# First block of a convolution and SiLU kernel: the copy of the taps on ScalarE instead of VectorE, and one product of zeros fewer

## The chip, the cores and the metric

The kernel runs on one core of a Trainium2 chip. The core has a matrix engine (TensorE, PE in the profile, with its weight loads as PEld), VectorE (DVE), ScalarE (ACT), GpSimd (POOL) and a queue engine (SyncE, SP) that only issues DMAs here. The engines run side by side, each takes its own instructions in order, and they wait for one another by semaphores. The metric is the time of one execution on the device in microseconds (us), less is better.

## What is computed

The input x is 8 sequences of 4096 tokens with 192 features, the output 32768 rows of 192. First a causal convolution of 7 taps along each sequence, with taps that are a softmax per head (8 heads of 24 features), then a two-layer block with SiLU between:

```python
def _attn_ref(x, weight):            # x (8, 4096, 192), weight (8, 7)
    w = np.exp(weight - weight.max(-1, keepdims=True))
    w = w / (np.sum(w, axis=-1, keepdims=True) + 1e-09)
    x_pad = np.concatenate([np.zeros((B, 6, D)), x], axis=1)
    idx = np.arange(S)[:, None] + np.arange(7)[None, :]
    x_unf = x_pad[:, idx, :].reshape(B, S, 7, H, 24)
    return np.einsum('hk,bskhg->bshg', w, x_unf).reshape(B, S, D)

def _moe_ref(x, w_in, w_out):        # w_in (192, 2048), w_out (2048, 192)
    h = x @ w_in
    return (h * (1.0 / (1.0 + np.exp(-h)))) @ w_out
```

The weights w_in and w_out are given in float64, all else in float32.

## The kernel before

The 32768 tokens are worked on in 32 blocks of 1024 tokens, each as two halves of 512. The features are split into three groups k of 64 (lines 120 to 150 load them); a tile xt holds both halves, 64 features on partitions 0 to 63 for the first 512 tokens and on 64 to 127 for the second, with 6 halo columns in front. VectorE transposes each loaded group into xt (turn_in, line 387). The convolution of a group multiplies shifted views of xt by one scalar per partition, the tap, which stands in the tile taps, 128 partitions by 3 x 7.

In all blocks but the first, a fixed plan written out in the kernel (PLAN) interleaves the convolution of the next block on VectorE with the products of this one on TensorE, the sums and SiLU. Blocks after the first use a product scheme with fewer multiplications (lines 497 and 570). The first block has no block before it to hide behind, and its start is written out by hand. Almost every instruction passes through a small helper, Pinned, which records it with an order to keep; all such instructions carry the line of that helper, L111, in the profile, so they are told apart by engine, operation and tile. Each engine's final sequence comes out of a scheduler; instructions with different engines are tied by semaphores alone.

The start of the first block, in steps:

- SP and ScalarE issue the first loads: weight, the four pieces of group 0 of x (tile nat), the halo of group 0 (halo, line 146), w_in for the rounding (tile raw), then the pieces of groups 1 and 2.
- VectorE clears zeros, warm, wown and one_hot. TensorE multiplies zeros by zeros into an unused bank (heat, line 339): four such products ahead of the taps and two behind them. Each shows as two records in the profile.
- POOL builds hot, a matrix of ones and zeros that maps heads to partitions, by six affine selects, and one_hot, an identity, by two, and clears the halo of the first half of xt.
- The softmax of weight runs on VectorE and ScalarE into wown. One product (line 365) of hot and wown puts the tap of the right head on each partition, into a bank by_head.
- by_head is copied to taps.
- diagonal (line 798) makes, for groups 0 and 1 and each tap, a diagonal 128 x 128 matrix on ScalarE: one_hot times the tap. conv_pe (line 805) uses these as weights: the convolution of groups 0 and 1 of the first block is 7 products for each half in TensorE, added up in a bank. Group 2 is done by VectorE (conv, lines 404 and 409) and spread by DMA (line 421).
- After the first transpose VectorE clears the halo columns of groups 1 and 2 on the upper 64 partitions, and POOL issues the DMAs that fill them (halo, line 146).
- VectorE and ScalarE round w_in, held as pairs of 32-bit words, to float32 tiles wr (rounded, round_in), in parts: three for the first of four, then the others whole; POOL copies them crosswise to ws.
- up_plain (line 460) does the first layer of the first block in four parts, down_plain (line 599) the second layer.

The hand-written sequence in question, after the functions:

```python
    turn_in(0, 0)
    vec.memset(xts[0][R:P, 1:NK, 0:pad], 0.0)
    for k in range(1, NK):
        halo(k, nc.gpsimd)
    diagonal(0)
    conv_pe(0)
    round_in(0, 0)
    diagonal(1)
    turn_in(0, 1)
    conv_pe(1)
```

Of the kernel before, what the change touches and what calls it, by code (L numbers as in the profile page):

```python
# [17 lines left out]
def kernel(  # L18
# [84 lines left out]
    def pin(ins):  # L103
        return tc.keep_in_program_order(ins)
# [8 lines left out]
    vec, act = Pinned(nc.vector), Pinned(nc.scalar)  # L113

    def bank():
        return psum.tile([P, TB], F32, tag="ps", name="ps")
# [219 lines left out]
    def heat(times):  # L336
        for _ in range(times):
            pin(
                nc.tensor.matmul(  # L339
                    idle[:, 0 : 2 * P],  # L340
                    zeros,
                    zeros.unsqueeze(1).to_broadcast([P, 2, P]),
                    start=True,
                    stop=True,
                )
            )

    idle, by_head = bank(), bank()[:, 0 : NK * K]
    taps = const.tile([P, NK, K], F32, name="taps")
# [20 lines left out]
            stop=True,  # L370
        )
    )
    heat(2)
    vec.tensor_copy(taps.rearrange("p k i -> p (k i)"), by_head)

    tails = {}

# [535 lines left out]
```

## Time and profile before

| what | value |
|---|---|
| median of four runs | 2409.5 us (2409.09, 2409.33, 2409.66, 2410.03) |
| the profiled execution, its own time | 2409.09 us |
| its span, first to last instruction | 2407.4 us |
| TensorE busy | 2399.6 us, 17878 records |
| VectorE busy | 2062.2 us |
| ScalarE busy | 995.1 us |
| POOL busy | 71.5 us |
| products of zeros (L339), first four, second two | 1.14 us for 3.61, 5.04 us for 1.11 |
| product that spreads the taps (L365) | 4.83 us for 0.37 |
| copy of the taps, VectorE | 5.23 us for 0.18 |
| first transpose, VectorE (L387) | 5.42 us for 0.71 |
| first seven diagonals, ScalarE | 5.51 us for 2.15 |
| products of the convolution (L805) | 6.28 us for 12.29, 56 records |

The page calls an engine busy while it has an instruction under way; matmuls overlap, so that a busy TensorE need not run at its peak, and the distance from one product's start to the next tells more than a product's length. "Idle before" with an arrow names what the profile takes for the event that ended a wait. In the chain of waits each piece is followed by what it released. Times are from the start of the span.

### The profile page before, as it was taken

How to read it: one execution, taken by the hardware profiler on the slowest of the kernel's cores; microseconds unless marked ns; L12 is line 12 of the kernel's file. 1: busy time of each engine (PE TensorE's matmuls, PEld its weight loads, DVE VectorE, ACT ScalarE, POOL GpSimd, SP SyncE). 2: the span in 40 equal slices, each digit the busy share in tenths (PEclk: the TensorE clock that was granted, in tenths of full speed). 3: DMA queues.
4: the chain of work that ended last, by engine and by line, in shares of the span. 5: the costliest groups of instructions: out<-in, count | busy, mean ns of one | idle time of the engine just before them, and what ended most of it. 6: DMA issues, size and time to landing. Idle time of an engine off the chain costs nothing.

```text
span 2407.4 us, 43335 instructions
## 1 busy us (share of the span) xinstructions
PE 2399.6 (100%) x17878; PEld 945.2 (39%) x17878; DVE 2062.2 (86%) x2812; ACT 995.1 (41%) x1873; POOL 71.5 (3%) x99
## 2 busy tenths in 40 slices
PE   9999999999999999999999999999999999999998
PEld 5333443334433344333344333443334433334433
DVE  8789888888888898888988888888889888898876
ACT  5334543334533345433454334453334533345432
POOL 4300000000000000000000000000000000000000
PEclk9999999999999999999999999999999999999999
DMA  7322122221222222222222222122222222222220
GB/s 159 61 45 47 34 36 54 54 41 32 44 45 54 40 41 36 44 54 44 45 37 36 54 51 43 32 40 50 53 40 41 36 45 54 43 43 37 38 40 14
DMA packets 453718, 110.59 MB, mean 46 GB/s; under 512 B 424080, under 2 KB 429200, under 8 KB 453520
## 3 DMA queue, kind: packets, MB, share of 16 engines
q1 hardware_dynamic: 449872, 105.85, 24.0%
q8 instruction: 140, 2.29, 0.4%
q0 software_dynamic: 448, 1.58, 0.3%
q10 hardware_dynamic: 3200, 0.39, 0.1%
q14 instruction: 58, 0.48, 0.1%
HBM read 31.46 MB, written 25.17 MB: 24 GB/s over the span
## 4 chain that ended last, share of the span: by engine, by line
PE 100%; DVE 0%; ACT 0%; issue 0%; ACTq 0%; DVEq 0%
PE ps L497 49%; PE ps L570 47%; PE ps L599 2%; PE ps L460 2%; PE ps L805 1%; PE ps L339 0%; DVE cmb L111 0%; ACT u L111 0%; DVE osb L111 0%; DVE xt L387 0%; PE ps L365 0%; ACTq L739 0%; DVE zeros L111 0%; DVE xt L111 0%; DVEq L387 0%
## 5 line engine op out<-in xcount | busy, mean ns | idle before, releaser
L497 PE MATMUL ps<-dup,ws 64*128 64x512 f32 x2480 | 869.9, 589 | 0.0
L570 PE MATMUL ps<-g,wo 128*32 128x512 f32 x2976 | 661.8, 593 | 0.0
L521 DVE TENSOR_TENSOR g<-u,ps 128x512 f32<-128x512 f32 x744 | 485.9, 680 | 119.1 <-PE ps L497 89.8
L497 PE MATMUL ps<-win,wr 64*128 64x512 f32 x1488 | 567.7, 589 | 0.0
L570 PE MATMUL ps<-t,wo 128*32 128x128 f32 (+2 forms) x4528 | 500.6, 446 | 0.0
L518 ACT ACTIVATE g<-g 128x512 f32<-128x512 f32 x744 | 444.7, 631 | 97.3 <-DVE g L521 97.3
L497 PEld LDWEIGHTS ps<-dup,ws 64*128 64x128 f32 x2480 | 363.0, 187 | 292.0 <-issue 277.7
L570 PE MATMUL ps<-t,wx 128*32 128x512 f32 x2976 | 452.7, 592 | 0.0
L409 DVE SCALAR_TENSOR_TENSOR nat<-xt,taps,nat 128x512 f32<-128x512 f32 x564 | 423.4, 751 | 18.3 <-ACT nat L404 3.7
L497 PE MATMUL ps<-dup,wr 64*128 64x512 f32 x992 | 419.9, 596 | 0.0
L512 ACT COPY u<-ps 128x512 f32<-128x512 f32 x496 | 278.1, 589 | 228.7 <-PE ps L497 225.8
L638 ACT COPY cmb<-ps 96x512 f32<-96x512 f32 x30 | 17.5, 582 | 805.3 <-PE ps L570 805.3
L538 DVE TENSOR_TENSOR t<-g 128x1024 f32<-128x1024 f32 x248 | 299.7, 1219 | 27.2 <-PE ps L570 27.2
L538 DVE TENSOR_TENSOR t<-g,t 128x1024 f32<-128x1024 f32 x248 | 303.3, 1224 | 13.6 <-PE ps L570 3.2
L497 PEld LDWEIGHTS ps<-win,wr 64*128 64x128 f32 x1488 | 233.4, 187 | 175.5 <-issue 146.9
L570 PEld LDWEIGHTS ps<-t,wo 128*32 128x32 f32 x4528 | 180.3, 110 | 219.8 <-issue 199.5
L497 PE MATMUL ps<-win,ws 64*128 64x512 f32 x496 | 242.2, 589 | 0.0
L570 PE MATMUL ps<-g,wx 128*32 128x512 f32 x1488 | 234.5, 592 | 0.0
L570 PEld LDWEIGHTS ps<-t,wx 128*32 128x32 f32 x2976 | 121.9, 110 | 278.8 <-issue 269.5
L650 DVE TENSOR_TENSOR cmb<-cmb,ps 96x512 f32<-96x512 f32 x150 | 102.3, 682 | 135.2 <-ACT u L635 133.1
L497 PEld LDWEIGHTS ps<-dup,wr 64*128 64x128 f32 x992 | 160.5, 187 | 128.2 <-issue 114.3
L570 PEld LDWEIGHTS ps<-g,wo 128*32 128x32 f32 x2976 | 168.5, 110 | 98.3 <-issue 98.3
(72 smaller groups left out, 1228.7 us busy)
## 6 DMA issues: line engine op xcount, KB each, us to landing
dup<-nat SPq DMA_DIRECT2D x376, 128.0 KB, 2.3
nat<-in_x_dram SPq DMA_DIRECT2D x382, 64.0 KB, 2.4
out_dram<-osb SPq DMA_DIRECT2D x376, 64.0 KB, 2.0
raw<-in_moe_w_out_dram SPq DMA_DIRECT2D x8, 384.0 KB, 3.9
raw<-in_moe_w_in_dram SPq DMA_DIRECT2D x12, 192.0 KB, 4.5
ws<-wr POOLq DMA_DIRECT2D x8, 192.0 KB, 4.0
raw<-in_moe_w_in_dram SPq DMA_DIRECT2D x6, 128.0 KB, 3.0
xt<-xt SPq DMA_DIRECT2D x31, 4.5 KB, 1.9
```

The lines of the kernel that those rows point to most:

```text
L409: nc.vector.scalar_tensor_tensor(out=dst, in0=src, scalar=tap, in1=dst, op0=ALU.mult, op1=ALU.add)
L460: nc.tensor.matmul(hs[a, n, e], rows(wr[j], e)[:, a, k, :], rows(d, e)[:, n, k, :], start=k == 0, stop=k == NK - 1,)
L497: nc.tensor.matmul(bk[b, m, bn], rows(w, half), rows(v, half), start=first, stop=True, skip_group_check=True,)
L512: pin(copy(u, bk[b, m, "1"]))
L518: pin(nc.scalar.activation(g, g, AF.Silu))
L521: pin(nc.vector.tensor_tensor(g, us.pop((b, m, i)), bk[b, m, bn], op=ALU.add))
L538: pin(nc.vector.tensor_tensor(t[i // 2][:, i % 2, :], u, v, op=ALU.subtract))
L570: nc.tensor.matmul(accs[b][at][SQ * q : SQ * q + SQ, to], lhs[:, e, SQ * k : SQ * k + SQ], rhs[:, e, ts(q, TB // 4) if i == 5 else to], st ...
L599: nc.tensor.matmul(acc[k][R * n : R * n + R, :], wo[j][:, a, e, R * k : R * k + R], gs[b, j, a][:, n, e, :], start=j == 0 and a == 0 and e ...
L638: pin(nc.scalar.copy(c[0], acc[0][0:n, :]))
L650: pin(nc.vector.tensor_tensor(out_, u, v, op=ALU.add))
L805: nc.tensor.matmul(by_pe[k][n], rows(diag, n)[:, k, i, :], rows(xts[0], n)[:, k, i : i + TB], start=i == 0, stop=i == K - 1,)
```

## The change

Two lines of the first block's start are changed. The second run of products of zeros has one in place of two. The copy of by_head to taps is issued on ScalarE in place of VectorE.

```diff
-    heat(2)
-    vec.tensor_copy(taps.rearrange("p k i -> p (k i)"), by_head)
+    heat(1)
+    act.copy(taps.rearrange("p k i -> p (k i)"), by_head)
```

In the built program, the sequences of the engines differ in these places and no other:

- TensorE: one product of zeros less between line 365 and line 805.
- VectorE: wown, then the first transpose, with no copy between.
- ScalarE: the exponential of weight, then the copy of by_head, then the first diagonal.
- POOL: the last of the six selects of hot stands behind the first of the two halo DMAs (line 146), where it stood ahead of it.
- SP: one of the loads of the second block's input stands ahead of a pair of loads of w_out, where it stood behind it.

POOL's queue from the last but one select of hot on, before and after:

```
before                                        after
select  hot<-hot                              select  hot<-hot
memset  xt                                    memset  xt
select  hot<-hot                              DMA     xt<-in_x_dram  (waits for VectorE)
DMA     xt<-in_x_dram  (waits for VectorE)    select  hot<-hot
DMA     xt<-in_x_dram                         DMA     xt<-in_x_dram
```

## The prediction

> **What bounds the kernel now.** I read the page's busy times first, then the waits of TensorE, then the chain that ended last in order of time, then the first 30 us of the timeline, engine by engine.
>
> Page, busy times; waits of TensorE over the whole span (engine, tile and line, releaser, us in total, times, longest):
>
> ```profile
> PE 2399.6 (100%) x17878; PEld 945.2 (39%) x17878; DVE 2062.2 (86%) x2812; ACT 995.1 (41%) x1873; POOL 71.5 (3%) x99
> ```
>
> ```profile
> PE ps L339 <- DVE warm L111: 1.1, 1, 1.1
> ```
>
> TensorE is busy for 2399.6 of 2407.4 us and has one listed wait, for its very first product. A late start of its work is therefore a late end, unless something later makes it wait anyway. The chain (start, length, what) shows where that work starts:
>
> ```profile
> 4.75 0.08 issue
> 4.83 0.39 PE ps L365 x2
> 5.21 0.02 issue
> 5.23 0.03 DVE taps L111
> ...
> 5.42 0.71 DVE xt L387
> 6.13 0.06 issue
> 6.19 0.08 DVE xt L111
> 6.27 0.01 issue
> 6.28 12.29 PE ps L805 x56
> ```
>
> ```profile
> 18.57 41.22 PE ps L460 x192
> 59.79 41.35 PE ps L599 x192
> ```
>
> From 6.28 on the chain is TensorE alone: 41.22 us over 192 products is 0.215 us each, 41.35 again, and each later block repeats 37.97 + 36.22 us to the hundredth. So the time of the kernel is the start of the first convolution product (line 805) plus a constant. The chain ahead of it: the product that spreads the taps over partitions (line 365, 4.83), VectorE's copy of them (5.23), VectorE's first transpose (5.42 to 6.13), the convolution. ScalarE's first diagonal (started 5.51, 0.386 us, so done at 5.90) is ready before the transpose. The POOL row that follows must be read beside it (timeline):
>
> ```profile
> 3.53 0.29 POOL L111 TENSOR_SCALAR_AFFINE_SELECT hot<-hot 32x128 f32<-32x128 f32 x1
> 6.57 1.53 POOL L146 DMA_DIRECT2D xt<-in_x_dram  x2 [2.75 <-DVE xt L111]
> ```
>
> ```profile
> 3.99 0.69 DVE L111 TENSOR_SCALAR wown<-wexp,wred 8x7 f32<-8x7 f32 x3
> 6.19 0.07 DVE L111 MEMSET xt<- 64x12 f32 x1
> ```
>
> The select at 3.53 is the last that builds hot, an operand of the line 365 product. The two halo DMAs come after it on POOL and wait for VectorE's memset at 6.19.
>
> **The change part by part.** Taken at its word, it lets the transpose start when VectorE is free (3.99 + 0.69 = 4.68) instead of behind the tap copy, and gives ScalarE the copy that ScalarE alone waits for. But the built order of POOL's queue changes with it. Before: memset xt, select hot, halo DMA, halo DMA. After: memset xt, halo DMA, select hot, halo DMA. The first halo DMA still waits for VectorE's memset, and that memset still stands behind the transpose. The last select of hot, so the line 365 product, so the taps, so the diagonals, now stand behind both. The old order could not be built this way (the memset stood behind the tap copy, which needs hot); the new one can. The path, step by step:
>
> - Transpose: starts 4.70. Its four loads must have landed: the second of SP's two is issued by about 1.7, and these loads land 2.9 us after issue in the median, 3.4 at most, so 4.6 to 5.1. I take 4.70, as the bytes of small packets thin out by 3.5 us. Ends 4.70 + 0.71 = 5.41.
> - Memset: 0.06 later, 0.07 long (6.13 to 6.19, 6.26): ends 5.54.
> - First halo DMA on POOL: 0.31 after the memset (6.26 to 6.57), issue 0.82: 5.85 to 6.67.
> - Last select of hot: POOL goes on 0.02 after the end of its DMA issues (35.81 + 1.31, next row 37.14), 0.29 long: ends 6.98.
> - Line 365 product: 0.15 after its last operand (4.68 to 4.83): 7.13. Taps can be read 0.40 later (4.83 to 5.23): 7.53.
> - Tap copy on ScalarE: no row has it. Nearest below: VectorE's same copy, 0.181, and ScalarE on 128x1, 0.204; above: ScalarE on 128x128, 0.386. For 21 columns I interpolate 0.23; bounds 0.18 and 0.39. Ends 7.76. The diagonal, which waits for it on the same engine, 0.05 later (the lag of VectorE's dependent rows, 3.76 to 3.80): 7.81.
> - First diagonal 0.386: 8.20; product 0.14 after (6.13 to about 6.28, the transpose being the wait): 8.34.
>
> Shift: 8.34 - 6.28 = 2.06 us. With the loose ends (load +0.4, copy -0.05 to +0.16, the lags -0.1 to +0.1) 1.9 to 2.7.
>
> The removed product of zeros costs or saves nothing here: the products of zeros no longer end anywhere near the wait, TensorE stands still until 8.34 in any case. Without that cover (the order of POOL as before) it would still have been hidden behind the transpose (the zeros ended at 5.04 + 1.11 = 6.15, against 6.13 for the transpose).
>
> What else is late: ScalarE's diagonals run 2.30 late (5.51 to 7.81), the rounding steps of w_in queued behind them (7.70) to 10.0, and VectorE's step that waits for these (8.15) to 10.45. VectorE idles 0.80 before its third transpose (11.26, a load), so from there it is 2.30 - 0.80 = 1.5 late. The tightest need of TensorE is the second part of w_in: rounded at 27.51 + 0.96 = 28.47, wanted at 18.37 + 48 x 0.215 = 28.68. Both slide, to 29.97 and 30.74: the margin grows, and no new wait comes. The halo columns land about 3.1 us after issue: the first at 9.8 at the latest, wanted at 8.34 + 6.0 = 14.4; the second, issued by 7.8, at 10.9, wanted by ScalarE at 13.5. On SP one load of the second block's input goes ahead of a pair of w_out loads (28.46 and 35.57), some 0.5 us of issue; that w_out is rounded at 51.14.
>
> One cost has only bounds: the pace of TensorE. The eight records of zeros from 1.14 start 0.45 us apart ((4.28 - 1.14) / 7), the last three of the second four 0.21 apart (5.34, 5.55, 5.77). The pace doubled at about 5.2, after some 4.1 us of work without a gap over 0.1 us, while the granted clock is 1.00 in every stretch. In the changed kernel TensorE stands still from 4.75 to 7.13 and again before 8.34. Lower bound: the pace comes as before and stays, 0. Upper bound from these rows: the 4.1 us start over at 8.34, half of them lost, 2.0 us. I take 0, because the first four products (3.61 us) are nearly all that was there when the pace came.
>
> [...]
>
> Sum against the profiled execution: 2409.09 (span 2407.4 and 1.7 around it) + 2.06 = 2411.15. That execution is the lowest of the four; the median stands 0.4 above, so **2411.6** for the median.
>
> **The rivals.**
>
> *Held on POOL, and the fast pace lost.* As above, but the convolution starts at half pace. For: the starting work is cut into 3.61 us, a gap of 2.4, under 1 us, a gap of 0.4. Against: only 0.6 us of products were still to come when the pace doubled. Price 0 to 2.0: 2411.6 + 2.0 = 2413.6 at the full bound, typically 2412.5 to 2413.6. This is also the one way to a measurable loss: over 0.2% (4.8 us, about what a measurement of this kernel can tell from no change) it needs 4.8 - 2.06 = 2.75 us here, 5.5 us of convolution at half pace, more than the 4.1 that the trace shows.
>
> *The change does what it says: the POOL order does not bind.* Taps at 5.23 + 0.23 = 5.46, diagonal from 5.51, done 5.90, product at 6.04: 0.24 earlier. But then the second part of w_in comes last (28.47 + 0.14 = 28.61 against 28.68 - 0.24 = 28.44) and takes 0.17 back: 2409.3 to 2409.5, not slower than before. For: the select is 0.29 us of work and was idle time's neighbour; against: each engine's rows start in the built order everywhere in this trace, and the product's wait is for the last of POOL's ten steps.
>
> *A later wait absorbs the shift.* If VectorE or a load bound TensorE somewhere in the first two blocks, the end would slide by less, 2409.5 to 2411. Against: one listed wait, and 0.215 us per product throughout.
>
> **How the numbers follow.** Held on POOL with the pace as before 0.52 (2411.0 to 2412.2); held with the pace lost 0.31; as it says 0.12; absorbed 0.05. The time is that of the first, 2411.6. The range 2410.9 to 2413.9 takes in the first, most of the second and a little of the last: about 0.8. All but the far end of the second lie within 0.2% (2404.7 to 2414.3): faster 0.01, same 0.90, slower 0.09.
>
> **What would show it.** On POOL the halo DMA near 5.85 ahead of the last select of hot (near 6.7); the line 365 product near 7.1; the tap copy on ScalarE at 0.2 to 0.3 us; the convolution near 8.3; line 460 at 20.6 and 41.2 long as before; no new wait of TensorE. A first convolution longer than 12.29 us for its 56 records would show the lost pace, and the excess its price. The prediction is wrong if the select ends by 4 us, if the convolution starts before 7, or if a later block's 37.97 or 36.22 changes.

## The result and the profile after

| | before | changed |
|---|---|---|
| median | 2409.38 us (60 runs, 2409.01 to 2410.03) | 2412.87 us (40 runs, 2412.42 to 2414.18) |
| span of the profiled execution | 2407.4 us | 2411.9 us |
| the profiled execution's own time | 2409.09 us | 2413.64 us |

The ratio is 1.0016, 95% interval 1.0011 to 1.002: slower, by 3.5 us in the median and by 4.5 us in the two profiled executions, and still within the 0.2% that the forecast counts as the same. The 40 times fall in two groups with nothing between: 21 from 2412.42 to 2412.87, 19 from 2413.39 to 2414.18. The profiled execution is of the upper group.

First the page's busy times and TensorE's waits (engine, tile and line, releaser, us in total, times, longest):

```profile
PE 2402.2 (100%) x17876; PEld 942.3 (39%) x17876; DVE 2064.4 (86%) x2811; ACT 995.3 (41%) x1874; POOL 70.6 (3%) x99
```

```profile
PE ps L365 <- POOL hot L111: 2.1, 1, 2.1
PE ps L339 <- DVE warm L111: 1.1, 1, 1.1
```

TensorE has one wait that it did not have: the product that spreads the taps waits 2.1 us for hot, on POOL. The chain of waits tells what stood ahead of that on POOL (start, length, what):

```profile
4.67 0.71 DVE xt L387
5.38 0.06 issue
5.45 0.08 DVE xt L111
5.53 0.29 issue
5.82 0.82 POOL xt L146
6.64 0.06 issue
6.70 0.30 POOL hot L111
7.00 0.04 issue
7.04 0.62 PE ps L365 x2
7.66 1.03 PE ps L339 x2
8.69 14.43 PE ps L805 x56
```

```profile
23.12 41.20 PE ps L460 x192
64.32 41.35 PE ps L599 x192
```

Transpose, memset, halo DMA, select of hot, tap product: the order of POOL's queue, step after step. Two more things are in these lines. The 56 records of the convolution take 14.43 us where they took 12.29. And the chain comes to them from the product of zeros (line 339), not from ScalarE's diagonal. From line 460 on all is as before (41.20 and 41.35 against 41.22 and 41.35), 4.55 us later. So the whole loss lies before 23.12 us: 2.3 to 2.4 us in the start of the convolution (8.62 against 6.28 for its first record; 8.69 in the chain), 2.14 us in its length.

TensorE's weight loads show where the length comes from (timeline, start, length, gap before):

```profile
11.35 0.34 PEld L805 LDWEIGHTS ps<-xt,diag 64*128 64x128 f32 x2 [0.51 <-ACT diag L111]
12.20 0.34 PEld L805 LDWEIGHTS ps<-xt,diag 64*128 64x128 f32 x2 [0.51 <-issue]
13.05 0.22 PEld L805 LDWEIGHTS ps<-xt,diag 64*128 64x128 f32 x2 [0.51 <-ACT diag L111]
13.52 0.19 PEld L805 LDWEIGHTS ps<-xt,diag 64*128 64x128 f32 x2 [0.24 <-issue]
13.95 0.19 PEld L805 LDWEIGHTS ps<-xt,diag 64*128 64x128 f32 x2 [0.24 <-issue]
```

Up to 13.05 the pairs start 0.85 us apart, after that 0.43: TensorE runs at half pace for 4.4 us of the convolution. "ACT diag" as a releaser is not the reason; the diagonals come every 0.31 us, and the distance is the same where no releaser is named.

TensorE was at half pace already when it fell idle, and still when it went on (timeline, the first four products of zeros and the tap product):

```profile
1.14 3.78 PE L339 MATMUL ps<-zeros 128*128 128x256 f32 x8 [1.14 <-DVE warm L111]
7.04 0.62 PE L365 MATMUL ps<-wown,hot 96*128 96x21 f32 x2 [2.12 <-POOL hot L111]
```

In the profile before, the same rows took 3.61 and 0.37 us: there the full pace had come by the start of the tap product at 4.83.

### The profile page after: what moved, and what is told of

Same layout as the page of the kernel before. It is cut to its first block, busy times and chain, and to the rows that moved or that the text cites. A ratio compares the mean times of both kernels' runs of the same rounds, so it can differ in the third digit from the quotient of the medians.

```text
span 2411.9 us, 43332 instructions
## 1 busy us (share of the span) xinstructions
PE 2402.2 (100%) x17876; PEld 942.3 (39%) x17876; DVE 2064.4 (86%) x2811; ACT 995.3 (41%) x1874; POOL 70.6 (3%) x99
## 4 chain that ended last, share of the span: by engine, by line
PE 99%; DVE 0%; ACT 0%; issue 0%; POOL 0%; ACTq 0%; DVEq 0%
PE ps L497 49%; PE ps L570 46%; PE ps L599 2%; PE ps L460 2%; PE ps L805 1%; DVE cmb L111 0%; ACT u L111 0%; PE ps L339 0%; ACTq L128 0%; DVE osb L111 0%; POOL xt L146 0%; DVE xt L387 0%; PE ps L365 0%; DVE wown L111 0%; ACT L111 0%
```

## The experiments

My theory after the result: two causes, in a row. POOL's order holds the tap product back, and the standing still costs TensorE its full pace. The rivals: ScalarE's copy is to blame, or the missing product of zeros, or the pace has nothing to do with the waiting.

**e1, one product of zeros fewer, and nothing else**

```diff
-    heat(2)
+    heat(1)
     vec.tensor_copy(taps.rearrange("p k i -> p (k i)"), by_head)
```

> One product of zeros fewer, tap copy still on VectorE, every other queue as before. Theory (the loss comes from POOL's order and from the pace that the waiting costs): TensorE's standing still stays under 0.7 us, the convolution starts at 6.28 as before, 2409.4 us, no difference over 0.2 us. Rival (the removed product alone lets the pace slip): the convolution's 56 records take more than 12.3 us, and the time lies 0.5 to 2 us above before.

Measured 2409.23 against 2409.56 us for before beside it, ratio 1.0 (0.9991 to 1.0009); the convolution starts at 6.27 and takes 12.29 us. But two of the 11 times are 2411.10 and 2411.13, where none of the 33 of before is above 2410.22. The removed product is not what costs 3.5 us; it costs some 2 us in some executions. Theory and rival each had a part of it.

**e2, the copy on ScalarE, and nothing else**

```diff
     heat(2)
-    vec.tensor_copy(taps.rearrange("p k i -> p (k i)"), by_head)
+    act.copy(taps.rearrange("p k i -> p (k i)"), by_head)
```

> The tap copy on ScalarE, both products of zeros kept, POOL's order as in the changed kernel. Theory (POOL's order): the select of hot ends at 7.0, the convolution starts at 8.4 to 8.7, and the time is that of the changed kernel, 2412.4 to 2414.2 in two groups; one product more in the gap changes the pace little, so within 0.6 us of 2412.9. Rival (the removed product matters): back to 2411.5, the pace being kept by the second product.

Measured 2414.16 (2411.28 to 2414.51), ratio 1.0017 (1.0008 to 1.0026). POOL's rows are those of the changed kernel: DMA at 5.85, select at 6.73. So the move of the copy brings the loss. That the median lies 1.3 us above the changed kernel's was not expected, and the chain says why (before, the wait for POOL; here, what follows the tap product):

```profile
7.07 0.62 PE ps L365 x2
7.69 1.89 PE ps L339 x4
9.57 14.03 PE ps L805 x56
```

At half pace the two products of zeros take 1.89 us and end at 9.57, after the first diagonal (ScalarE starts it at 8.00); the convolution stands behind them. The changed kernel's one product ends at 8.69. One execution, 2411.28, is 1.6 us below the next: with no profile of it, I can only guess that it kept the pace.

**e3, the whole change with POOL's order restored.** The halo columns are first filled from the tap tile, not with zeros; the DMAs overwrite them either way. Since the taps need hot, the halo DMAs can only come after the select.

```diff
-    vec.memset(xts[0][R:P, 1:NK, 0:pad], 0.0)
+    vec.tensor_copy(xts[0][R:P, 1:NK, 0:pad], taps[R:P, 1:NK, 0:pad])
```

> The whole change, but the halo columns are first filled from the tap tile instead of with zeros (the DMAs overwrite them either way), which puts both halo DMAs behind the last select of hot as before. Theory (POOL's order is the whole cause): the convolution starts at 6.0 to 6.1 in place of 8.6, its 56 records take 12.3 us, and the time is 2409.2 to 2409.5. Rival (ScalarE's copy or the missing product is to blame): 2410.5 to 2413.

Measured 2409.10 against 2409.56, ratio 1.0 (0.9991 to 1.0008); again two times of 11 above 2411. The chain:

```profile
4.82 0.38 PE ps L365 x2
5.21 0.02 issue
5.23 0.19 ACT taps L111
...
5.50 0.41 ACT diag L111
5.91 0.04 issue
5.95 12.29 PE ps L805 x56
18.24 8.15 PE ps L460 x37
```

With the select in its old place (3.53) the loss is gone, with ScalarE's copy and one product of zeros still in. The copy does what it was said to: the transpose leaves the chain, the diagonal takes its place, and the convolution starts 0.33 us earlier than before. Part of that is given back: line 460's 192 records take 41.35 us in place of 41.22, with one weight load, at 28.39, coming 0.68 us after the end of the one before it, where the others come after 0.21 to 0.24. The rounded weights of line 460's second part, ready at 27.32 + 0.96 = 28.28, fit that wait; the profile names a step of ScalarE for it, so this is my reading. The span is 0.1 us shorter than before, which no time can tell from nothing.

**e4, the changed kernel with TensorE's wait filled**

```diff
-    heat(4)
+    heat(8)
```

> The changed kernel with eight products of zeros in place of four ahead of the taps' product, so that TensorE works on until about 6.7 while POOL holds it; POOL's order as in the changed kernel. Theory (the shift is 2.0 to 2.3 us of waiting plus 1 to 2 us of half pace): the convolution starts at 8.4, its records take 12.3 us, 2411.4 to 2411.7, and the two groups of times go. Rival (the pace has nothing to do with the idle time): the records still take 13.3 to 14.5 us, 2412.4 to 2414.

Measured 2411.12 (2410.98 to 2411.60; one group), ratio 1.0006 (0.9998 to 1.0015). POOL's order is that of the changed kernel (DMA 5.86, select 6.74), and the chain now goes through the zeros:

```profile
1.14 6.40 PE ps L339 x16
7.54 0.15 PE ps L365 x2
...
7.98 0.41 ACT diag L111
8.39 0.04 issue
8.43 12.29 PE ps L805 x56
```

Work that computes nothing makes the changed kernel faster: all 11 times lie below all 40 of the changed kernel, and the median is 1.56 us above that of before beside it, in place of 3.49. The convolution is back at 12.29 us, and it starts 0.19 us earlier, no longer behind zeros at half pace. What is left in the profile, 8.43 - 6.28 = 2.15 us, is POOL's order, with some 0.2 us of the added zeros in it: the tap copy starts at 7.71, where the select's end, 7.03, with 0.04 to the tap product as in the changed kernel and 0.40 to the copy as before, would give 7.47 (an estimate). The rival that the pace has nothing to do with the waiting falls.

**e5, order restored, both products of zeros kept**, e3 with `heat(2)`

> The order restored as in e3, and both products of zeros kept behind the taps' product. In e1 and e3, with one of them, 2 of 11 times each stand near 2411.1, some 2 us above the rest; of the 93 times of before none does. Theory (the second product of zeros covers the stretch before the convolution, and without it the fast pace is lost in some executions): no time above 2410.3; the convolution starts at 6.15 to 6.25 behind the zeros in place of 5.95, 2409.1 to 2409.5. Rival (the stray times have to do with the earlier convolution or the copy): again one or more near 2411.

Measured 2409.61 (2409.02 to 2410.26), ratio 1.0 (0.9992 to 1.0009): no stray time, and nothing gained, since the zeros now end last (convolution at 6.24 in the profile).

**e6, the kernel before with no product of zeros behind the tap product**

```diff
-    heat(2)
+    heat(0)
```

> The kernel before with no product of zeros behind the taps' product (four ahead of it kept); POOL and the tap copy as before. Theory (what keeps the pace is work without a gap up to the convolution): with 1.1 us of standing still before 6.28 the fast pace is lost in more executions than in e1, a third or more of the times 1 to 2 us above 2409.4, the rest at 2409.1 to 2409.7. Rival (the four products ahead are enough): all at 2409.0 to 2410.2.

Measured 2410.89, in two groups: five times from 2409.05 to 2409.31, six from 2410.89 to 2411.37. The profiled execution, 2411.30, is of the upper group:

```profile
4.82 0.59 PE L365 MATMUL ps<-wown,hot 96*128 96x21 f32 x2
6.49 14.23 PE L805 MATMUL ps<-xt,diag 64*128 64x512 f32 x56 [1.08 <-DVE xt L111]
```

A gap of 1.08 us is enough here, where the pace is still at half (the tap product takes 0.59 us): 14.23 us for the convolution. With no, one and two products of zeros in that gap, 6 of 11, 4 of 22 (e1 and e3 together) and none of 11 (e5) executions go slow, and none of the 81 of before beside all these runs is above 2410.22. The rival, that the four products ahead are enough, falls.

**e7, the kernel before with no product of zeros at all**

```diff
-    heat(4)
+    heat(0)
 ...
-    heat(2)
+    heat(0)
```

> The kernel before without any product of zeros, all else as before. The price of half pace by itself: the convolution starts at 6.2 to 6.3, its first 3.5 to 6.5 us run at half pace, its 56 records take 14 to 15.5 us in place of 12.3, and the time is 2411 to 2412.6. If the pace did not depend on earlier work, 2409.4.

Measured 2411.24 (2410.84 to 2412.36), as expected; the convolution takes 14.63 us from 6.46. This is the price of a start at half pace by itself: 1.4 to 3.0 us above before's 2409.41. The changed kernel's half pace (2.14 us in its profile) is of that size.

**e8, order restored, one product of zeros and one of half its columns**

```diff
-    heat(1)
+    heat(1); pin(nc.tensor.matmul(idle[:, 0:P], zeros, zeros, start=True, stop=True))
```

> The order restored as in e3, one product of zeros behind the taps' product, and a second one of 128 columns in place of 256, to fill TensorE's wait for the first diagonal without delaying the convolution. Theory: convolution at 5.95 to 6.0, no time near 2411, 2409.0 to 2409.2: at or just below before. Rival: stray times near 2411 as in e3.

Measured 2409.16 (ten times from 2408.80 to 2409.73, one at 2411.60), ratio 0.9999 (0.9991 to 1.0008). The convolution starts at 5.96 and takes 12.29 us. Still one stray time: between this and e3 the runs decide nothing, and neither beats the kernel before beyond its interval.

**e9, the whole change, the two halo DMAs on SP**

```diff
-        halo(k, nc.gpsimd)
+        halo(k, nc.sync)
```

> The whole change, with the two halo DMAs issued from SP in place of POOL; nothing of VectorE is touched, its memset stays. They stand behind SP's last small load of w_in there. Theory (the halo DMA ahead of the select is the cause, wherever it goes instead): the select of hot ends at 3.8, the convolution starts at 5.95 to 6.1, 2409.0 to 2409.5 with a stray time or two near 2411 as in e3. Two costs could show: the halo lands later (issued near 11, landed by 14.5, wanted by TensorE at 12.1), which would make TensorE wait up to 2.5 us at half of the second group and bring 2410 to 2411.6. Rival (the memset or the tap copy is the cause): convolution at 8 or later.

Measured 2411.09 (2411.00 to 2411.25), ratio 1.0007 (0.9998 to 1.0016). The convolution starts at 5.96: the halo DMA ahead of the select is the cause, whichever way it is taken out. But on SP it stands behind other loads, and TensorE pays later:

```profile
PE ps L460 <- DVE wr L111: 0.8, 1, 0.8
PE ps L805 <- DMA xt<-in_x_dram: 0.6, 1, 0.6
```

The weight load for the second group waits 1.44 us for the halo (at 13.70; the line above counts only where TensorE itself ran dry), and VectorE, 1.1 us later with its group (15.3 against 14.2 in the changed kernel, 12.81 before), makes TensorE wait 0.8 us for the rounded w_in at 31.07. What moves out of a queue must land in one with room.

**e10 and e11, the changed kernel again**, for a profile from the lower group of its times

> The changed kernel once more, for a profile from the other group of its times (2412.4 to 2412.9). Theory: the same start at 8.6, but the 56 records take 13.2 to 13.5 us in place of 14.4, the fast pace coming some 2 us sooner. Rival: the groups differ in the start of the convolution.

> As the run before: a second draw for a profile from the group at 2412.4 to 2412.9, with 13.2 to 13.5 us for the 56 records and the start at 8.6.

Both missed: 2413.72 and 2413.37, with the start at 8.65 in both and 14.44 and 14.11 us for the 56 records. The lower group has no profile. Its times, 0.8 to 1.2 us below the profiled 2413.64, would fit 1.5 to 2.4 us less at half pace than that profile's 4.4 (an estimate), but this wasn't seen.

## Why the prediction was right, and where it was wrong

The time lies in the range, and the mechanism that the forecast rests on is shown: POOL's order holds the tap product (waits, chain, e3, e9). The case that came was however its first rival, held and the pace lost, and not the one that I called likeliest. The single value, 2411.6, is 1.3 us low; the range held because that rival had been counted into it.

- *POOL's order.* Right step by step: halo DMA 5.82 (5.85 forecast), select done 6.99 (6.98), tap product 7.04 (7.13), tap copy on ScalarE 0.18 long (0.23, and 0.18 was the lower bound).
- *"The pace of TensorE ... I take 0".* This is the step that failed. It measured 2.14 us in the profile, above the bound of 2.0, and e4 shows that the standing still is its cause. The reading under it was off as well: in the profile before, the pace had doubled by 4.83 and not at about 5.2, as the tap product's 0.37 us shows, and the 4.1 us of the bound are no fixed length here (last section). The reason given, that the first four products were nearly all that was there when the pace came, read too much into one execution: in the changed kernel's profile the same four run at half pace to their end, and e6, which has them too, goes slow in 6 of 11.
- *"The removed product of zeros costs or saves nothing here."* Wrong too. At half pace a product of zeros takes some 0.9 us (two take 1.89 in e2) and the convolution queues behind it; with two of them (e2) it starts at 9.5, with one at 8.6, without half pace (e4) at 8.43. The removal saves 0.9 us in the held kernel. With the select in its old place, one product in place of two goes with some 2 us more in 4 of 22 executions (e1 and e3), where the forecast had the second one hidden behind the transpose at no price.
- *The start of the convolution, 8.34.* 8.62 in the profile: 0.19 are the zeros; and from the tap product to the tap copy it is 0.66 us in place of 0.40, the product being at half pace (0.62 long against 0.39). e4, at full pace but held a little longer by its own zeros, has 8.43. Two lags of the sum were misread and make up for some of it: the product follows the diagonal by 0.04 us (8.39 to 8.43 in e4) and not by 0.14, because in the chain before it followed the memset and not the transpose; and the tap product follows the select by 0.04 and not by 0.15.
- *As it says.* The rival's first half held once the order was restored: 0.33 us earlier (0.24 forecast), and w_in's second part takes some of it back, as worked out.
- *The 0.2%.* Right, narrowly: the ratio is 1.0016, the upper end of its interval 1.002. But the forecast also took 0.2% for about the least that a measurement of this kernel can tell from no change, and 0.16% was told from it: all 40 times lie above all 60 of before.

How long TensorE must work before the full pace comes, these runs leave open. In e6's profile it works without a gap from 1.14 to 5.41, 4.27 us, and is still at half pace after a 1.08 us gap (14.23 us for the convolution); in the profile before the tap product at 4.83, 3.69 us after the start of the first product, runs at full pace (0.37 us). That a pace that has come outlives a gap of 2.1 us, no run here shows: the three profiles of the changed kernel are all of executions in which it had not come. What halves the pace, no row names.

## What to carry to other kernels

When an instruction moves to another engine, compare the built order of every queue, also of those that the diff does not name: here one copy less on VectorE let a scheduler put a DMA that waits ahead of 0.29 us of work that everything needs. Where a matrix engine is the bound from its first product on, as here, let filler work reach up to the first real product: here none of 11 executions (e5) and one of 11 (e8) went slow where it did in the profile, 4 of 22 where it ended 0.56 or 0.24 us short (e1, e3), and 6 of 11 with 1.08 us left empty (e6). The price shows only in some executions, so that a few runs can miss it. And filler at half pace stands in the way of what it is meant to prepare: in e2 two products behind the taps took 1.89 us, and the convolution began at 9.51, against 8.62 behind one in the changed kernel.

## What the runs showed of the hardware

- The granted clock reads 0.999 or 1.00 in every run here, and 1.00 also from 8.62 to 13.05 us of the changed kernel, where TensorE runs at half pace: the distance of starts (0.85 against 0.43 us a pair) shows it, the clock row does not.
- With one or no product of zeros behind the taps (e1, e3, e6) one and the same kernel gives 2408.8 to 2409.4 or 2410.9 to 2411.4, nothing between. The profiles of e1 and e3, both of the lower group, show the convolution at full pace (12.29 us), that of e6, of the upper, has half pace at its start (14.23). That half pace is decided anew in each execution is my reading of this.
- The wait for full pace had no fixed length here. By the distances of starts it came 4.0 us after the work without a gap began in e6 (at 6.49), 5.4 in e11 (at 7.07) and 6.1 in the changed kernel (at 7.04). From lengths alone, as estimates, it was 3.2 us in e3 (its first four products take 3.48 us, in the changed kernel at half pace 3.78: 3.78 - 2 x 0.30) and 4.7 in e7 (twice the 2.34 us that its convolution takes above 12.29).
- In these profiles half pace reached far into the convolution only where TensorE stood still before full pace had come. Of the 12 profiles with products of zeros ahead of the taps, five have full pace by 4.83 us (before, e1, e3, e8, e9) and keep it over gaps of up to 0.6 us. Of the other seven, e4 and e5 work on until it has come, and their convolutions take 12.29 us; the changed kernel's three, e2 and e6 stand still for 1.08 to 2.16 us, and theirs take 14.0 to 14.4.
- The changed kernel's 42 times leave 2412.9 to 2413.3 empty, and none is near the 2411.0 to 2411.6 of e4, where the pace is full. Why there are two groups stays open.
